# Batches 2 to 7: Q, K and x turned by TensorE in place of DMA transposes, in a fused attention and MLP kernel

## The chip, the cores and the metric

The kernel runs on one core of one Trainium2 chip. Its engines are TensorE (PE: matrix products out of SBUF into PSUM), VectorE (DVE), ScalarE (ACT), GpSimd (POOL) and SyncE (SP, which here only issues DMAs). Each engine works through its own queue in order, and they wait for each other through semaphores. The metric is device time in microseconds (us) of one execution, taken as the median of a few runs. A profile is one execution more, with every instruction's start and duration.

## The reference

Block-causal attention over 8 batches of 8 heads, 576 tokens and 64 dimensions, and then a gated MLP on the joined heads of all 4608 tokens:

```
scores = q @ k.T / sqrt(64)            # masked: block_i >= block_j, blocks of 64
attn   = softmax(scores);  a = attn @ v
x      = a.transpose(0, 2, 1, 3).reshape(4608, 512)
h      = x @ w_in                      # 512 -> 2048
g      = h * sigmoid(beta * h)
out    = g @ w_out                     # 2048 -> 512, float32
```

## The kernel before

**Attention.** The work is cut into 32 units u = 4 * batch + c, one for each batch and pair of heads. TensorE contracts over the partitions, so Q and K must stand with the head dimension on the partitions (tile `QKT`), while they arrive with tokens there. For each unit: scores (line 818, two heads at a time on the two halves of the array), Exp on ScalarE (lines 839 and 854), small memsets on VectorE for the mask, attention times V with a column of ones for the row sums (`fav`, line 882), a reciprocal and a multiplication on VectorE (lines 894 and 901, the normalisation) into `xq`. Then `xq`, with tokens on the partitions, is turned into `xT`, with features on the partitions, which is what the MLP needs.

**How Q and K are turned.** Batches 0 and 1 (`b < QB`) load Q and K in pieces (`fl`, line 711), cast them to bf16 on GpSimd (two on VectorE; line 718), turn them with TensorE into a PSUM bank (line 727, four transposes a piece; the 64 tokens left over in lines 656 and 688) and copy them to `QKT` on VectorE (line 735). Batches 2 to 7 load half a batch's heads at once (line 749), cast in four steps on GpSimd (lines 763 and 767) and turn all of it with one DMA transpose that SP issues (line 774): 2816 columns of 128, which is 22 blocks of 128 x 128.

**How x is turned.** Batches 0 to 2 (`b < XB`) use five TensorE transposes a unit (line 930) and a copy (VectorE in line 940; ScalarE in line 938 for units 2 and 3). Batches 3 to 7 use DMA transposes that SP issues (line 918, one or two a unit, as the ring `xT` wraps).

**MLP.** Nine chunks of 512 rows. For each, 16 products of 512 columns (`fh`, line 1119, four matmuls each), Tanh on ScalarE (line 1129), and the gate on VectorE (line 1133, SCALAR_TENSOR_TENSOR). The product with `w_out` is plain for chunk 0 (line 1155), and for chunks 1 to 8 made from seven products of half size (line 1040) with additions on VectorE (line 1004).

**What sets the order.** Nothing is ordered by hand. A list scheduler (`Plan.schedule`, line 85) simulates the engines at build time with a cost for each step (`dur`, `lat`), and takes on each engine the ready step of the lowest priority number. The resulting order is fixed in the program, with the semaphores that it needs (`assign`). Further fields of a step steer it: `after` (not before that other step has been placed), `rest` (a margin behind its inputs), `tiles` (buffers that must be free: class `P1` is one of eight PSUM banks, `PP` a pair of them). Up to 50 us of planned time, TensorE's gaps are filled with idle matmuls that compute nothing that is used (lines 446 and 534). MLP chunks interleave with the attention of later batches: attention of batch b runs ahead of the chunks by the offset `LAG` in `pr(u)`, line 441.

Attention matmuls and MLP matmuls share TensorE, and the copies out of PSUM share VectorE and ScalarE with the gate and the softmax.

Of the kernel before, what the change touches and what calls it, by code (L numbers as in the profile page):

```python
# [10 lines left out]
B, H, S, D = 8, 8, 576, 64  # L11
# [348 lines left out]
def bass_blockwise_causal_attn__then__act_swish_beta_kernel(  # L360
# [10 lines left out]
    with es:  # L371
# [1 line left out]
            return es.enter_context(nc.sbuf_tensor(name, shape, dt))  # L373

        NQ = 2
        QB, XB, CAST = 2, 3, "POOL"
        NE = 3
        PARTS = [((0, 4, "SP", (4, 5, 0, 1, 2, 3)), (4, 8, "SP", range(2)), (4, 8, "POOL", (4, 5, 2, 3)))] + [((0, 8, "SP", range(6)),)] * 7
        GROUPS = [((0,), (1,), (2,), (3,))] + [((0, 1), (2, 3))] * 7
# [78 lines left out]
        def mk(fn):  # L458
            return lambda g, e: fn(g)
# [13 lines left out]
        for i in range(NQ):  # L473
            for h in range(2):
                vzero.append(P.op("DVE", 150, mk(lambda g, i=i, h=h: g.memset(
                    Vn[i][64 - 64 * h:128 - 64 * h, 4, h:8:2, 0:64], 0.0)), prio=-7))
                vzero.append(P.op("DVE", 300, mk(lambda g, i=i, h=h: g.memset(
                    Vs[i][64 - 64 * h:128 - 64 * h, 4, h:8:2, :], 0.0)), prio=-8))
            o = P.op("POOL", 200, mk(lambda g, i=i: g.memset(Vn[i][:, 4, :, 64:66], 0.0)), prio=-5)
            ones.append(o)  # L480
            ones.append(P.op("POOL", 200, mk(lambda g, i=i: g.memset(Vn[i][:, 0:4, :, 64:65], 1.0)), prio=-5))
            for h in range(2):
                ones.append(P.op("POOL", 100, mk(lambda g, i=i, h=h: g.memset(
                    Vn[i][64 * h:64 * h + 64, 4, h:8:2, 64:65], 1.0)), deps=[o], prio=-4))
            ones.append(P.op("POOL", 100, mk(lambda g, i=i: g.memset(Ef[i][:, 3136:3200], 0.0)), prio=-4))
        for i in range(NQ, NE + 1):
            ones.append(P.op("POOL", 100, mk(lambda g, i=i: g.memset(Ef[i][:, 3136:3200], 0.0)), prio=-4))


        bt = P.op("SP", 100, lambda g, e: [g.dma_start(betaT, moe_beta.rearrange("(j p) -> j p", p=128))],  # L490
# [112 lines left out]
            return z  # L603


        def blocks(b):
            x0 = S * b % RX
            n = min(5, (RX - x0) // 128)
            return [z for z in ((0, n, x0), (n, 5 - n, 0)) if z[1]]

        xt = []
        early6 = []
        TC = "POOL"
        QX = 2052
        QKI, QKX = 550, 3078
        for u in range(NU):
# [8 lines left out]
            if b < QB:  # L625

                if c == 0:
# [39 lines left out]
                    else:  # L667
# [21 lines left out]
                            return z  # L689

                        o = P.op("PE", 4 * 56, ft, deps=[*tails, c4], tiles=[tq, pe_], lat=4 * 56 + 170, mode="full", prio=pr(u) + .05)
                        o.rest = 700.0 if b else 0.0
                        tailc = []
                        for a in range(2):
                            def fc(g, e, pe_=pe_, td=quads[a][1], a=a):
                                y = QKT[td.slot][:, 0, 512:576]
                                y = bass.AP(y.tensor, y.offset, [y.ap[0], [1408, 2], [768, 2], [1, 64]])
                                return g.tensor_copy(y,
                                                     PSb[:, pe_.slot, 0:512].rearrange("c (w p a n) -> c a p w n", w=2, p=2, a=2)[:, a])

                            tailc.append(P.op("DVE", dve_t(256), fc, deps=[o], tiles=[pe_, quads[a][1]], prio=-5 if b < 1 else .5))
                if p == 0:
                    tn, tt_ = quads[c // 2]
                    tail = tailc[c // 2]
                turned = []
                for w, (nm, src) in enumerate((("Q", q), ("K", k))):
                    ts, pt = P.tile("ST"), P.tile("P1")
                    early6.append(ts)

                    def fl(g, e, ts=ts, src=src, b=b, c=c):  # L710
                        return [g.dma_start(STm[ts.slot].rearrange("p h j d -> p h (j d)"),
                                            src[b, 2 * c:2 * c + 2, 0:512].rearrange("h (p j) d -> p h (j d)", j=4))]

                    o = ld[nm, u] = P.op("SP", 420 if b else 500, fl, tiles=[ts], xfer=750 if b else 820, prio=u, dma=["d_S", 0, 1])
                    o.pkt = 63.0

                    def fn(g, e, ts=ts, tn=tn, p=p, w=w):
                        return g.tensor_copy(QKn[tn.slot][:, p, 768 * w:768 * w + 512].rearrange("p (j h d) -> p j h d", j=4, h=2),
                                             STm[ts.slot].rearrange("p h j d -> p j h d"))

                    onp = u not in (0, 3) or w == 1
                    o = P.op("POOL" if onp else "DVE", 620 if onp else 430, fn, deps=[o], tiles=[ts, tn],
                             prio=-40 + 3 * u if onp else -1)

                    def ft(g, e, tn=tn, pt=pt, p=p, w=w):
                        for i in range(4):
                            z = g.transpose(PSb[:, pt.slot, 128 * i:128 * i + 128],
                                            QKn[tn.slot][:, p, 768 * w + 128 * i:768 * w + 128 * i + 128], identB[:])
                        return z

                    o = P.op("PE", 4 * 56, ft, deps=[o, c4], tiles=[tn, pt, tt_], lat=4 * 56 + 170, mode="full",
                             prio=pr(u))

                    def fc(g, e, pt=pt, td=tt_, p=p, w=w):
                        return g.tensor_copy(QKT[td.slot][:, p, 768 * w:768 * w + 512].rearrange("c (p j) -> c p j", j=4),
                                             PSb[:, pt.slot, 0:512].rearrange("c (j p) -> c p j", j=4))

                    o.rest = 700.0 if b else 0.0

                    if u == 1:  # L740
                        o.after = fq0
                    turned.append(P.op("DVE", dve_t(512) + 30, fc, deps=[o], tiles=[pt, tt_], prio=-5 if b < 1 else .5))
            elif p == 0:

                for w, (nm, src) in enumerate((("Q", q), ("K", k))):
# [24 lines left out]

                        casts.append(P.op(CAST, 740 if w else 1000, fn, deps=[o], tiles=[ts, tn], prio=u))

                def ft(g, e, tn=tn, td=tt_):
                    return [g.dma_start_transpose(QKT[td.slot][:].rearrange("c a (t n) -> c (a t) n", n=128),
                                                  QKn[tn.slot][:].rearrange("p a n -> p (a n)"))]

                turned = [P.op("SP", 3500, ft, deps=casts, tiles=[tt_, tn], xfer=3762, prio=-1, dma=["d_T", 0, 1])]
            tqk, cps = tt_, turned
            more = [tail] if b < QB else []
            ex = []  # L780
# [1 line left out]
            if b not in JOIN or p == 0:  # L782
# [4 lines left out]
                for grp in visits:  # L787
# [3 lines left out]
                    def fq(g, e, pst=pst, grp=grp, tqk=tqk, b=b):  # L791
                        keep = {}
                        for (uu, g0), ps in zip(grp, pst):
# [4 lines left out]
                            for t, q0, q1, off in blocks:  # L798
# [25 lines left out]
                    o = P.op("PE", n, fq, deps=cps + (more if b or grp[0][1] > 0 else []), tiles=list({id(x): x for x in pst}.values()) + [tqk] + [tes[uu] for uu in sorted({uu for uu, _ in grp})] * (b > 0),  # L824
                             lat=n + 200, mode="row", prio=pr(u) + .2 if len(grp) == 4 else pr(u + 1) + .1 if grp[0][0] > u else
                             pr(u) + .1 + .1 * (grp[0][1] >= 2))
                    if u == 0 and grp[0][1] == 0:
                        fq0 = o
                    for (uu, g0), ps in zip(grp, pst):
# [47 lines left out]
            def fav(g, e, te=te, pv=pv, Tv=Tv, c=c):  # L877
                for h in range(2):
                    for i in range(5):
# [6 lines left out]
            av = P.op("PE", 30 * 34, fav, deps=ex + zs + load[u], tiles=[te, Tv, pv, ti, tx],  # L886
                      lat=30 * 34 + 180, mode="full", prio=pr(u)+.4 + 5 * (b < 1))

            def both(pv, n0, n1):
                a = PS[:, pv.slot, n0:n1]  # L890
                return bass.AP(a.tensor, a.offset, [a.ap[0], [512, 2], [65, 5], [1, n1 - n0]])
# [21 lines left out]
                m = P.op("DVE", dve_t(640), fm, deps=[av, r], tiles=[pv, ti, tx], prio=-6 if b < 1 else 0)  # L913
                m.same = [r]
            nrm = [m]
            if b >= XB:
                def fy(g, e, tx=tx, c=c, b=b):
                    return [g.dma_start_transpose(
                        xT[:, c, x0:x0 + 128 * n].rearrange("c (t n) -> c t n", n=128),
                        xq[xq_(tx)][:, t0:t0 + n, :].rearrange("p t n -> p (t n)")) for t0, n, x0 in blocks(b)]  # L920

                n = len(blocks(b))
                xt.append(P.op("SP", 1000 * n, fy, deps=nrm + (xt[u - 4:u - 3] if b > XB else []), tiles=[tx], xfer=855,
                               prio=-1, dma=[f"d_TX{n}_", 0, n]))
                continue
            px = P.tile("P1")

            def fx(g, e, tx=tx, px=px):
# [3 lines left out]

            xp = P.op("PE", 5 * 57, fx, deps=nrm, tiles=[tx, px], lat=5 * 57 + 170, mode="full", prio=pr(u)+.5 + 5 * (b < 1))

            def fy(g, e, px=px, c=c, b=b):
                for t0, n, x0 in pieces(b):
                    if e == "ACT":
                        z = g.activation(xT[:, c, x0:x0 + n], PSb[:, px.slot, t0:t0 + n], ACT.Copy)
                    else:
                        z = g.tensor_copy(xT[:, c, x0:x0 + n], PSb[:, px.slot, t0:t0 + n])  # L940
                return z
            xt.append(P.op("ACT" if u in (2, 3) else "DVE", 600 if u in (2, 3) else 520, fy, deps=[xp], tiles=[px], prio=-6 if u < 4 else 0))

        for o in P.ops:
            if o.idx > 40 and o.engs == ("PE",) and not o.fill and any(d.engs == ("SP",) or d.engs == ("POOL",) for d in o.deps) and not o.rest:
# [162 lines left out]
        for r in range(NRC):  # L1108
# [26 lines left out]
                gs.append(P.op("DVE", dve_t(512), fg, deps=[a] + (spare.users + spare_x.users if r == 1 else []), tiles=[ph, tt, tg], prio=0))  # L1135

            for b in range(B):
                if any((S * b + a) // RC - RX // RC == r for a in (0, S - 1 if b < XB else 639)):
                    for c in range(4):
                        xt[4 * b + c].deps += hs  # L1140

# [107 lines left out]
```

## Time and profile before

| | us |
|---|---|
| runs before (3) | 333.79, 329.07, 334.52; median 333.79 |
| profiled execution, its own time | 332.46 |
| its span, first to last instruction | 330.6 |
| SP's DMA transposes: QKT <- QKn, 12, median issue to landing | 7.2 |
| SP's DMA transposes: xT <- xq, 24, median issue to landing | 2.7 |
| TensorE transposes L727 (64) and L930 (55 of 60 with source xq), busy | 6.5 and 4.9 |
| VectorE copies L735 (16 of 512 columns), busy | 11.0 |

How to read it: a page gives for each engine the time in which one of its instructions was running, as a share of the span. A group of instructions is a line of the program, with the mean duration of one and the idle time of the engine just before it. "PEld" are TensorE's weight loads, which overlap its matmuls. "SPq" and "POOLq" are DMA-issuing instructions, whose length is that of the issue and not of the transfer. Matmuls are pipelined: one takes longer than the distance to the next.

### The profile page before, as it was taken

To read this page: it belongs to the slowest core of one execution; us is meant where nothing else is said; L and a number is where in the kernel's file an instruction comes from. 1 tells how busy PE (TensorE), PEld (TensorE's weight loads), DVE (VectorE), ACT (ScalarE), POOL (GpSimd) and SP (SyncE) were. 2 spreads that over 40 slices of the span, in tenths; PEclk is the share of its full clock that TensorE was granted. 3 is DMA by queue.
4 is the path that set the end of the run, shared out by engine and by line. 5 is a ranking of instruction groups with operands and counts; after the bars stand their busy time and mean duration, and the time that the engine had idled before them with its cause. 6 is when DMAs were issued, how large, how long until landed. Compare 5 with 4: busy or idle time off the path is not lost.

```text
span 330.6 us, 7365 instructions
## 1 busy us (share of the span) xinstructions
PE 317.3 (96%) x3062; PEld 197.5 (60%) x2979; DVE 220.3 (67%) x454; ACT 211.8 (64%) x316; POOL 91.5 (28%) x155
## 2 busy tenths in 40 slices
PE   7898999999999999999989999899999999999996
PEld 1363464435677557845655577655566766666685
DVE  5765883777754897367967684289576866666742
ACT  3857964396737976687678855676978445554521
POOL 5962290084183066003910650080000000000000
PEclk9999999999999999999999999999999999999999
DMA  7999999999899999959899999895030310111023
GB/s 221 251 227 238 205 241 197 204 260 234 187 300 215 207 229 217 234 112 217 173 180 184 235 264 205 202 209 110 0 73 2 103 34 32 33 64 35 3 92 129
DMA packets 147442, 54.20 MB, mean 164 GB/s; under 512 B 116672, under 2 KB 146896, under 8 KB 147408
## 3 DMA queue, kind: packets, MB, share of 16 engines
q1 hardware_dynamic: 132560, 40.72, 61.9%
q0 software_dynamic: 5568, 4.36, 8.4%
q10 hardware_dynamic: 9280, 8.65, 7.9%
q8 instruction: 24, 0.39, 0.5%
q14 instruction: 10, 0.08, 0.1%
HBM read 36.71 MB, written 9.44 MB: 140 GB/s over the span
## 4 chain that ended last, share of the span: by engine, by line
PE 64%; DMA 11%; SPq 8%; DVE 6%; POOL 4%; ACT 3%; issue 2%; POOLq 0%; ACTq 0%
PE PS L1119 25%; PE PS L1040 25%; SPq L560 5%; PE PS L818 5%; DMA ST<-in_q_dram 5%; PE PS L882 5%; DMA w_out<-in_moe_w_out_dram 4%; DVE gT L1133 2%; PE PS L1155 2%; ACT E L839 2%; POOL QKn L767 1%; DMA xT<-xq 1%; DVE xq L901 1%; DMA OV<-in_v_dram 1%; POOL Vn L587 1%
## 5 line engine op out<-in xcount | busy, mean ns | idle before, releaser
L1119 PE MATMUL PS<-xT,w_in 128*128 128x512 bf16 x540 | 129.9, 379 | 3.9 <-POOL QKn L763 1.1
L1129 ACT ACTIVATE th<-PS,beta 128x512 f32<-128x512 f32 x144 | 96.6, 701 | 54.4 <-PE PS L1119 49.8
L1133 DVE SCALAR_TENSOR_TENSOR gT<-th,PS 128x512 f16<-128x512 f32 x144 | 95.5, 681 | 34.9 <-ACT th L1129 34.1
L839 ACT ACTIVATE E<-PS 128x1024 bf16<-128x1024 f32 x93 | 92.1, 1031 | 14.6 <-PE PS L818 12.0
L1119 PEld LDWEIGHTS PS<-xT,w_in 128*128 128x128 bf16 x576 | 53.3, 98 | 56.9 <-DVE gT L1133 2.0
L1040 PE MATMUL PS<-w_out,gT 128*128 128x256 f16 x512 | 62.7, 273 | 0.0
L1040 PEld LDWEIGHTS PS<-w_out,gT 128*128 128x128 f16 x512 | 49.3, 98 | 11.0 <-issue 0.4
L587 POOL CAST Vn<-Vs 128x640 bf16<-128x640 f32 (+1 forms) x28 | 20.6, 734 | 101.8 <-DMA Vs<-in_v_dram 100.5
L1061 ACT ACTIVATE ost<-PS 128x512 f32<-128x512 f32 x32 | 19.2, 600 | 30.3 <-PE PS L1040 30.3
L882 PEld LDWEIGHTS PS<-Vn,E 128*128 128x128 bf16 x930 | 31.3, 97 | 5.7 <-DVE E L845 1.8
L882 PE MATMUL PS<-Vn,E 128*128 128x65 bf16 x930 | 32.5, 193 | 1.5 <-DMA xT<-xq 1.5
L818 PE MATMUL PS<-QKT 64*64 64x64 bf16 (+4 forms) x328 | 33.9, 295 | 0.0
L1040 PE MATMUL PS<-OV 128*128 128x256 f16 x256 | 32.3, 273 | 0.0
L767 POOL CAST QKn<-ST 128x384 bf16<-128x384 f32 x48 | 27.2, 594 | 5.5 <-DMA ST<-in_q_dram 2.8
L818 PEld LDWEIGHTS PS<-QKT 64*128 64x128 bf16 (+1 forms) x328 | 13.2, 96 | 25.4 <-issue 10.4
L1040 PEld LDWEIGHTS PS<-OV 128*128 128x128 f16 x256 | 24.0, 98 | 6.9 <-issue 1.9
L901 DVE TENSOR_TENSOR xq<-PS,inv 128x640 bf16<-128x640 f32 x31 | 25.3, 820 | 0.5
L1004 DVE TENSOR_TENSOR OV<-gT 128x1024 f16<-128x1024 f16 x32 | 22.6, 711 | 1.0 <-PE PS L1040 0.4
L845 DVE MEMSET E<- 64x64 uint32 x62 | 6.9, 112 | 22.0 <-ACT E L839 20.0
L1064 DVE SCALAR_TENSOR_TENSOR ost<-PS,ost 128x512 f32<-128x512 f32 x22 | 15.2, 689 | 9.0 <-PE PS L1040 4.5
L763 POOL CAST QKn<-ST 128x640 bf16<-128x640 f32 x24 | 18.8, 784 | 4.9 <-DMA ST<-in_k_dram 3.3
L1155 PE MATMUL PS<-w_out,gT 128*128 128x512 f16 x64 | 16.0, 380 | 0.5 <-DMA w_out<-in_moe_w_out_dram 0.5
(77 smaller groups left out, 185.0 us busy)
## 6 DMA issues: line engine op xcount, KB each, us to landing
out_dram<-ost ACTq DMA_DIRECT2D x32, 256.0 KB, 3.7
ST<-in_q_dram SPq DMA_DIRECT2D x12, 576.0 KB, 6.2
ST<-in_k_dram SPq DMA_DIRECT2D x12, 576.0 KB, 7.2
Vs<-in_v_dram SPq DMA_DIRECT2D x24, 256.0 KB, 4.3
ST<-in_q_dram SPq DMA_DIRECT2D x8, 256.0 KB, 6.2
ST<-in_k_dram SPq DMA_DIRECT2D x8, 256.0 KB, 6.5
w_in<-in_moe_w_in_dram POOLq DMA_DIRECT2D x4, 512.0 KB, 11.3
w_out<-in_moe_w_out_dram POOLq DMA_DIRECT2D x4, 512.0 KB, 10.6
```

Source lines behind the costliest of these rows:

```text
L587: return g.tensor_copy(Vn[t.slot][:, 0:n, g0:g1, 0:64], Vs[ts.slot][:, 0:n, g0:g1, :])
L767: z = g.tensor_copy(QKn[tn.slot][:, a, 384 * i:384 * i + 384].rearrange("p (t h d) -> p t h d", t=3, h=2), x)
L818: z = g.matmul(o, QKT[tqk.slot][r, uu % 2, 768 + 128 * t + y:768 + 128 * t + m + y], x)
L839: return g.activation(y, x, ACT.Exp, scale=0.125)
L882: z = g.matmul(o, eblk(te, t, i, h), Vn[Tv.slot][:, t, 2 * c + h, 0:65], start=(t == 0), stop=(t == i))
L901: return g.tensor_tensor(xq[xq_(tx)][:].rearrange("p i (h d) -> p h i d", h=2), both(pv, 0, 64), x, ALU.mult)
L1004: return P.op("DVE", dve_t(SZ * HC / 2), mk(lambda g: g.tensor_tensor(fo(), fx(), fy(), op)), deps=deps, tiles=tiles, prio=prio)
L1040: x = g.matmul(PS[:, pw.slot, HM * w:HM * w + HM], fa()[:, j, 128 * w:128 * w + 128], fb()[:, j, :], start=first and (pair or w == 0) and ...
L1119: z = g.matmul(PS[:, ph.slot, :], w_in[:, c, 128 * j:128 * j + 128], xT[:, c, row % RX:row % RX + RC], start=(c == 0), stop=(c == 3))
L1129: return g.activation(th[tt.slot][:], PS[:, ph.slot, :], ACT.Tanh, scale=beta[:, j:j + 1])
L1133: return g.scalar_tensor_tensor(out=gT[tg.slot][:, j, :], in0=th[tt.slot][:], scalar=1.0, in1=PS[:, ph.slot, :], op0=ALU.add, op1=ALU.mult)
L1155: z = g.matmul(PS[:, po.slot, 0:d1 - d0], gT[tg.slot][:, j, 128 * w:128 * w + 128], w_out[:, j, d0:d1], start=(j == 0), stop=(j == NJ - 1))
```

## The change

- `QKT` of batches 2 to 7: the DMA transpose goes. In its place TensorE turns the 22 blocks into three PSUM banks (8, 8 and 6 blocks, `TURN`), and VectorE, ScalarE and VectorE copy them to `QKT`.
- `xT` of batches 3 to 7: the DMA transpose goes, and with it `XB` and `blocks`; these batches take the path of line 930. The copy is on ScalarE for units of odd number from 5 on, otherwise on VectorE.
- Batch 0: the copies of x for units 0 and 1 go from VectorE to ScalarE, where those of units 2 and 3 were.
- Batch 1: the VectorE copies of its turned Q and K are planned only after the normalisation of unit 3 (`last0["m"]`); its turns rest 400 instead of 700 ns. For unit 3 too, the turn now comes after the first scores of the unit before it.
- GpSimd's memsets at the start have other planned costs; those of 155 are planned behind the first K cast.
- The dependence between `xT`'s ring and the MLP uses the last token that is written (`S - 1`) for all batches.

```diff
-        QB, XB, CAST = 2, 3, "POOL"
+        QB, CAST = 2, "POOL"
+        TURN = ((0, 8, "DVE"), (8, 16, "ACT"), (16, 22, "DVE"))
...
-            o = P.op("POOL", 200, mk(lambda g, i=i: g.memset(Vn[i][:, 4, :, 64:66], 0.0)), prio=-5)
+            o = P.op("POOL", 150, mk(lambda g, i=i: g.memset(Vn[i][:, 4, :, 64:66], 0.0)), prio=-5)
...
-                ones.append(P.op("POOL", 100, mk(lambda g, i=i, h=h: g.memset(
+                ones.append(P.op("POOL", 155, mk(lambda g, i=i, h=h: g.memset(
                     Vn[i][64 * h:64 * h + 64, 4, h:8:2, 64:65], 1.0)), deps=[o], prio=-4))
...
+                    if u == 0 and w == 1:
+                        for x in ones:
+                            if x.dur < 160:
+                                x.after = o if x.dur > 150 else None
...
-                    o.rest = 700.0 if b else 0.0
-
-                    if u == 1:
-                        o.after = fq0
+                    o.rest = 400.0 if b else 0.0
+
+                    if u in (1, 3):
+                        o.after = fqs[u - 1, 0]
                     turned.append(P.op("DVE", dve_t(512) + 30, fc, deps=[o], tiles=[pt, tt_], prio=-5 if b < 1 else .5))
+                    turned[-1].after = last0["m"] if b else None
...
-                def ft(g, e, tn=tn, td=tt_):
-                    return [g.dma_start_transpose(QKT[td.slot][:].rearrange("c a (t n) -> c (a t) n", n=128),
-                                                  QKn[tn.slot][:].rearrange("p a n -> p (a n)"))]
-
-                turned = [P.op("SP", 3500, ft, deps=casts, tiles=[tt_, tn], xfer=3762, prio=-1, dma=["d_T", 0, 1])]
+                turned = []
+                for n0, n1, eng in TURN:
+                    pt = P.tile("P1")
+
+                    def ft(g, e, tn=tn, pt=pt, n0=n0, n1=n1):
+                        x = QKn[tn.slot][:].rearrange("p a n -> p (a n)")
+                        for i in range(n0, n1):
+                            z = g.transpose(PSb[:, pt.slot, 128 * (i - n0):128 * (i - n0) + 128],
+                                            x[:, 128 * i:128 * i + 128], identB[:])
+                        return z
+
+                    n = n1 - n0
+                    o = P.op("PE", n * 56, ft, deps=casts, tiles=[tn, pt, tt_], lat=n * 56 + 170, mode="full", prio=pr(u))
+
+                    def fc(g, e, td=tt_, pt=pt, n0=n0, n1=n1):
+                        y = QKT[td.slot][:].rearrange("c a n -> c (a n)")[:, 128 * n0:128 * n1]
+                        x = PSb[:, pt.slot, 0:128 * (n1 - n0)]
+                        return g.activation(y, x, ACT.Copy) if e == "ACT" else g.tensor_copy(y, x)
+
+                    turned.append(P.op(eng, act_t(128 * n) if eng == "ACT" else dve_t(128 * n), fc, deps=[o],
+                                       tiles=[pt, tt_], prio=.5))
...
-            if b >= XB:
-                def fy(g, e, tx=tx, c=c, b=b):
-                    return [g.dma_start_transpose(
-                        xT[:, c, x0:x0 + 128 * n].rearrange("c (t n) -> c t n", n=128),
-                        xq[xq_(tx)][:, t0:t0 + n, :].rearrange("p t n -> p (t n)")) for t0, n, x0 in blocks(b)]
-
-                n = len(blocks(b))
-                xt.append(P.op("SP", 1000 * n, fy, deps=nrm + (xt[u - 4:u - 3] if b > XB else []), tiles=[tx], xfer=855,
-                               prio=-1, dma=[f"d_TX{n}_", 0, n]))
-                continue
...
+            if u == 3:
+                last0 = {"av": av, "m": m, "xp": xp}
...
-            xt.append(P.op("ACT" if u in (2, 3) else "DVE", 600 if u in (2, 3) else 520, fy, deps=[xp], tiles=[px], prio=-6 if u < 4 else 0))
+            on = "ACT" if u in (0, 1, 2, 3) or u > 4 and u % 2 else "DVE"
+            xt.append(P.op(on, 600 if on == "ACT" else 700 if b > 1 else 520, fy, deps=[xp], tiles=[px], prio=-6 if u < 4 else 0))
...
-                if any((S * b + a) // RC - RX // RC == r for a in (0, S - 1 if b < XB else 639)):
+                if any((S * b + a) // RC - RX // RC == r for a in (0, S - 1)):
```

More of the change, by code (lines that the diff above doesn't have):

```diff
@@ L478, in bass_blockwise_causal_attn__then__act_swish_beta_kernel @@
                     Vs[i][64 - 64 * h:128 - 64 * h, 4, h:8:2, :], 0.0)), prio=-8))
-            o = P.op("POOL", 200, mk(lambda g, i=i: g.memset(Vn[i][:, 4, :, 64:66], 0.0)), prio=-5)
+            o = P.op("POOL", 150, mk(lambda g, i=i: g.memset(Vn[i][:, 4, :, 64:66], 0.0)), prio=-5)
             ones.append(o)
-            ones.append(P.op("POOL", 200, mk(lambda g, i=i: g.memset(Vn[i][:, 0:4, :, 64:65], 1.0)), prio=-5))
+            ones.append(P.op("POOL", 290, mk(lambda g, i=i: g.memset(Vn[i][:, 0:4, :, 64:65], 1.0)), prio=-5))
             for h in range(2):
-                ones.append(P.op("POOL", 100, mk(lambda g, i=i, h=h: g.memset(
+                ones.append(P.op("POOL", 155, mk(lambda g, i=i, h=h: g.memset(
                     Vn[i][64 * h:64 * h + 64, 4, h:8:2, 64:65], 1.0)), deps=[o], prio=-4))
-            ones.append(P.op("POOL", 100, mk(lambda g, i=i: g.memset(Ef[i][:, 3136:3200], 0.0)), prio=-4))
+            ones.append(P.op("POOL", 190, mk(lambda g, i=i: g.memset(Ef[i][:, 3136:3200], 0.0)), prio=-4))
         for i in range(NQ, NE + 1):
-            ones.append(P.op("POOL", 100, mk(lambda g, i=i: g.memset(Ef[i][:, 3136:3200], 0.0)), prio=-4))
+            ones.append(P.op("POOL", 190, mk(lambda g, i=i: g.memset(Ef[i][:, 3136:3200], 0.0)), prio=-4))
         bt = P.op("SP", 100, lambda g, e: [g.dma_start(betaT, moe_beta.rearrange("(j p) -> j p", p=128))],
@@ L603, in pieces @@
             return z
[L606 to L609, printed above, removed]
         xt = []
         early6 = []
+        fqs, avs = {}, {}
         TC = "POOL"
+        last0 = {}
         QX = 2052
@@ L701, in bass_blockwise_causal_attn__then__act_swish_beta_kernel @@
                             tailc.append(P.op("DVE", dve_t(256), fc, deps=[o], tiles=[pe_, quads[a][1]], prio=-5 if b < 1 else .5))
+                            tailc[-1].after = last0["m"] if b else None
                 if p == 0:
@@ L736, in fc @@
                                              PSb[:, pt.slot, 0:512].rearrange("c (j p) -> c p j", j=4))
-                    o.rest = 700.0 if b else 0.0
-                    if u == 1:
-                        o.after = fq0
+                    o.rest = 400.0 if b else 0.0
+                    if u in (1, 3):
+                        o.after = fqs[u - 1, 0]
                     turned.append(P.op("DVE", dve_t(512) + 30, fc, deps=[o], tiles=[pt, tt_], prio=-5 if b < 1 else .5))
+                    turned[-1].after = last0["m"] if b else None
             elif p == 0:
@@ L826, in bass_blockwise_causal_attn__then__act_swish_beta_kernel @@
                              pr(u) + .1 + .1 * (grp[0][1] >= 2))
+                    if b < 1:
+                        fqs[u, grp[0][1]] = o
                     if u == 0 and grp[0][1] == 0:
@@ L887, in bass_blockwise_causal_attn__then__act_swish_beta_kernel @@
                       lat=30 * 34 + 180, mode="full", prio=pr(u)+.4 + 5 * (b < 1))
+            avs[u] = av
+            if u == 3:
+                for x, y in ():
+                    avs[x].after = fqs[y]
             def both(pv, n0, n1):
@@ L933, in bass_blockwise_causal_attn__then__act_swish_beta_kernel @@
             xp = P.op("PE", 5 * 57, fx, deps=nrm, tiles=[tx, px], lat=5 * 57 + 170, mode="full", prio=pr(u)+.5 + 5 * (b < 1))
+            if u == 3:
+                last0 = {"av": av, "m": m, "xp": xp}
             def fy(g, e, px=px, c=c, b=b):
```

## The prediction, made before the run

> **What bounds the kernel now.** I read the page first, for the shares and the slices; then the busy times by stage, to see which stage has room on which engine; then TensorE's own waits; then the timeline, for what one transpose costs in this kernel. From the page:
>
> ```profile
> PE 317.3 (96%) x3062; PEld 197.5 (60%) x2979; DVE 220.3 (67%) x454; ACT 211.8 (64%) x316; POOL 91.5 (28%) x155
> PE   7898999999999999999989999899999999999996
> PEclk9999999999999999999999999999999999999999
> DMA  7999999999899999959899999895030310111023
> ```
>
> Two resources look full: TensorE from the second slice to the last but one, and the DMA engines up to slice 27 (some 225 us). The change takes work from the second and gives it to the first. So the question is which one sets the time. The stages (start; batch 1; batches 2 to 7; MLP alone; end), with TensorE busy, weight loads, VectorE, ScalarE, GpSimd, granted clock, DMA share and GB/s after each stretch's length:
>
> ```profile
> 0.00:27.20 27.20, 23.29 (x323) 10.99 (x262) 16.60 (x49) 15.90 (x24) 18.94 (x47) 1.00 1.07 234
> 27.20:60.00 32.80, 31.57 (x303) 16.33 (x298) 21.72 (x52) 21.43 (x32) 11.60 (x18) 1.00 1.17 218
> 60.00:262.00 202.00, 196.91 (x1969) 123.75 (x1945) 140.74 (x289) 144.64 (x215) 60.91 (x90) 1.00 0.90 182
> 262.00:313.00 51.00, 50.68 (x342) 33.77 (x346) 35.05 (x54) 26.16 (x39) 0.00 (x0) 1.00 0.12 42
> 313.00:330.60 17.60, 14.87 (x133) 12.63 (x130) 6.23 (x12) 3.67 (x6) 0.00 (x0) 1.00 0.30 105
> ```
>
> The last full stretch has hardly any DMA and TensorE is still full, so nothing that becomes free before it can shorten it. Busy time is a union of modelled durations and may hide slack, so I counted the work instead. The weight loads are recorded completely. From 262 to 313 they are 126 of line 1119 (512 columns) and 220 of line 1040 (256 columns). The timeline spaces eight of the first 1.73 us apart and eight of the second 0.87: 0.216 and 0.109 us each, 27.2 + 24.0 = 51.2 us of work in 51.0. That stretch is full. From 60 to 262: 384 x 0.216 = 82.9; 549 x 0.109 = 59.8; 720 attention-value matmuls at 0.91 per 30 = 21.8; twelve pairs of score units at 1.80 (visits of 0.54, 0.72 and 0.54) = 21.6; 32 of line 1155 at 0.216 = 6.9; 20 transposes at 0.056 = 1.1. Together 194.1 us in 202.0. So 7.9 us of holes, and 1.2 idle before 60, are all the room that TensorE has after 27 us.
>
> The Trainium skill ("Perfetto Trace Analysis", Identifying the Most-Contended Engine) warns that matmul busy share is a poor measure of how full TensorE is, and prefers weight-load busy share, here 60%. That would leave far more room than I allow; the count above disagrees.
>
> What TensorE waited for after 27.2 us until 313:
>
> ```profile
> PE PS L882 <- DMA xT<-xq: 1.5, 1, 1.5
> PE PS L1119 <- POOL QKn L763: 1.1, 1, 1.1
> PE PS L1119 <- DVE gT L1133: 0.7, 2, 0.5
> PE PS L1119 <- issue: 0.6, 4, 0.2
> PE PS L930 <- DVE xq L901: 0.6, 1, 0.6
> ```
>
> One wait of 1.5 us is on a DMA transpose. The 1.1 us are put down to a cast that line 1119 doesn't read; the xT transposes issued just before it are the likelier cause, which is an inference. All else that the DMA queue does is hidden: GpSimd waits 100.5 us for V and nobody waits for GpSimd.
>
> **What the change adds.** The price of a transpose comes from the timeline, where one block's start and the next block's start give the cost without the pipeline's tail:
>
> ```profile
> 29.35 0.39 PE L727 MATMUL PS<-identB,QKn 128*128 128x128 bf16 x4
> 29.57 1.03 PE L1119 MATMUL PS<-xT,w_in 128*128 128x512 bf16 x4
> ```
> ```profile
> 47.63 0.44 PE L930 MATMUL PS<-identB,xq 128*128 128x128 bf16 x5
> 47.91 1.07 PE L882 MATMUL PS<-Vn,E 128*128 128x65 bf16 x30
> ```
>
> Four take 0.22 us and five 0.28, so 0.056 each at a granted clock of 1.00. Added are 22 for each half of a batch's heads, 2 halves x 6 batches = 264, and 5 for each of the 20 units of batches 3 to 7 = 100. 364 x 0.056 = **20.4 us**, on the engine that has no room.
>
> The Trainium skill ("TensorE: Matmul & The Clock Gate", Back-to-back issue gap) gives about 81 ns for a 128-column matmul in a stream of weight load and matmul pairs. By it the addition would be 29.5 us and the time some 9 us above my sum. The two blocks above are such streams and show 56.
>
> The copies out of PSUM: VectorE's xT copies took 409 ns for 512 columns and 181 for 64, so 0.51 ns a column and 148 fixed: 670 for 1024 and 540 for 768. Twelve turns make 14.5 us, ten x copies at 0.59 make 5.9: 20.4 us. ScalarE's took 597 and 218, so 1.03 us for 1024: 12.4, and ten x copies at 0.815 make 8.2: 20.6 us. Over 60 to 262, grown by 20 us, VectorE goes from 70% to 73% and ScalarE from 72% to 74%. Neither becomes the bound; what hides the copies is that TensorE has other blocks queued. If that cover goes, TensorE waits for a bank. The nearest row is line 930's own wait: 0.6 us in 8 blocks after 27 us. For 36 turning blocks and 20 x blocks that is 56/8 x 0.6 = 4.2 us at the upper end. The lower end is 0, since line 727 has no idle time after 27 us in six blocks. I take the middle, **2.1**, because both rows are of the same form. Each new turn waits on TensorE for four GpSimd casts; everything behind it on TensorE's queue would wait too. The planner holds such a step 300 ns behind its casts, and the 1.1 us above is the largest such row. It lies within the 4.2.
>
> **What it takes away.** The 36 DMA transposes leave SP's queue and the loads behind them issue earlier. On TensorE that is worth the two waits, 1.5 + 1.1 = **2.6 us**. At least the 1.5 goes; at most all 7.9 + 1.2 = 9.1 us of holes.
>
> **The start.** First MLP matmul at 27.19. VectorE, before it:
>
> ```profile
> 23.45 0.68 DVE L735 COPY QKT<-PS 128x512 bf16<-128x512 bf16 x1
> 24.05 0.21 DVE L894 RECIPROCAL inv<-PS 128x10 f32<-128x10 f32 x1
> 24.17 0.63 DVE L735 COPY QKT<-PS 128x512 bf16<-128x512 bf16 x1
> 24.72 0.81 DVE L901 TENSOR_TENSOR gT<-PS,inv 128x640 bf16<-128x640 f32 x1
> ```
>
> The fourth attention-value block ends at 23.61. Its reciprocal waits for one batch 1 copy and its multiplication for another. With both behind it, the multiplication starts near 23.9: **0.8 us** earlier, and the transposes, ScalarE's copy and the first MLP matmul follow (its w_in had landed at 22.6). Moving the copies of units 0 and 1 to ScalarE (0.71 a unit) uses its idle 3.1 us before 24.68; put ahead of the last Exp, one could cost that 0.7 back, and VectorE, relieved of 0.97, could give another 0.4. So 0.1 to 1.2. The held batch 1 copies have cover until the scores at 27.93. Memsets: four on GpSimd (0.61 us) go behind the first K cast, which starts at 5.08 after K landed at 4.7. That is at most 0.3, and the chain of waits then runs through a Q load that lands at 9.07, so 0; the pushed memsets fit into the 1.19 us for which GpSimd next waits for a Q load. The shorter hold of batch 1's turns (400 for 700) and the smaller ring dependence touch no wait that TensorE shows: 0.
>
> **Sum.** 330.6 + 20.4 + 2.1 - 2.6 - 0.8 = 349.7 of span; 332.46 - 330.6 = 1.9 lie around it: 351.6. The profiled execution was 1.3 below the median of three, inside their scatter of 329.07 to 334.52, so I leave that out. **Predicted 351.5 us**, 5.3% slower. Ends: 330.6 + 20.4 + 0 - 9.1 - 1.2 + 1.9 = 342.6, and 330.6 + 20.4 + 4.2 - 1.5 - 0.1 + 1.9 = 355.5, with the 1.3 of the median 356.8. Range 343 to 357.
>
> **Rivals.** *Banks become the bound (slower still).* Eight PSUM banks serve scores, attention values, MLP and now 56 more blocks, whose copies stand in VectorE's and ScalarE's queues behind 0.7 to 1.0 us instructions. If each block cost the 0.35 us that one wait on line 1133 cost, it would be 19.6 us instead of 2.1: 369. It decides once copies come later than the next free bank; 73% and 74% busy speak against it, and so does line 930. Chance 9%.
>
> *TensorE was held by the DMA (not slower).* If DMA traffic delayed operands so that relieved matmuls ran closer, the transposes would fit. Place: 27 to 262 us. Price: it must give 20.4 us back for no change, or 13.7 for 2%. It decides if the matmuls there are spaced over 5% wider than alone. Against it: the same spacings, 0.216 and 0.109, account for 194.1 of 202.0 us with DMA at 0.90 and for all 51.0 with 0.12. Full recovery of every hole still ends at 342.6, 2.6% slower than the median; at 30 ns a transpose it would be 333. Chance 8%.
>
> That the change doesn't do what it says is no case: both places that issue the DMA transposes go.
>
> **Chances.** Forecast 83%, banks 9%, relief 8%. A measurement tells about 2% from no change. Relief splits into 2% faster and 6% within 2%; all else is slower, 92%.
>
> **What would show it.** Some 364 more transposes on TensorE, 0.055 to 0.06 apart; TensorE still at 96% or more, with 337 us busy; the stretch of pure MLP starting some 20 us later and still at the same spacing; VectorE and ScalarE near 241 and 234 us; DMA done well before 225 us with no gain from it; the first MLP matmul near 26.4. I'm wrong if a turning block costs over 0.1 us of TensorE idle, or if the work after 27 us ran closer than counted.

## The result, and the profile after

| | us |
|---|---|
| after, 4 runs | 352.44, 353.52, 352.44, 352.97; median 352.71 |
| before, 4 runs on the same chip | 329.07 to 334.52; median 332.20 |
| ratio after / before, 95% interval | 1.0655 [1.0556, 1.0754] |
| span of the profiled execution, before and after | 330.6 and 350.6 |

The change makes the kernel slower by some 20 us. The forecast was 351.5 in a range of 343 to 357. Before scatters by 1.6% and after by 0.3%, so the later comparisons, with 7 to 19 runs of before each and medians of 332.4 to 333.5, put the distance at 19 to 20 us. They ran on four chips, between which before's median differs by 1.1 us, so a difference of that size between kernels of different experiments says little.

From the page of the changed kernel (busy time with its share, the slices, and the large DMA queue):

```profile
PE 338.3 (96%) x3420; PEld 218.0 (62%) x3346; DVE 233.6 (67%) x488; ACT 234.2 (67%) x362; POOL 88.7 (25%) x155
PE   8999999899999999999999999999999999999996
DMA  7999999999959512961089200000000100020023
q1 hardware_dynamic: 84816, 28.78, 37.1%
```

The same queue in the kernel before:

```profile
q1 hardware_dynamic: 132560, 40.72, 61.9%
```

TensorE has 21.0 us more to do and is as full as before, over a longer span. The DMA engines, busy up to slice 27 before, now have holes from slice 12 on, and q1's share fell from 61.9% to 37.1%. Nothing of that shows in the time.

Busy time by stage, cut at the first MLP matmul and where the pure MLP stretch begins (TensorE, weight loads, VectorE, ScalarE, GpSimd, granted clock, DMA share, GB/s):

```profile
26.05:60.00 33.95, 31.80 (x326) 17.39 (x320) 22.40 (x50) 24.29 (x38) 12.21 (x19) 1.00 1.15 225
60.00:282.00 222.00, 217.74 (x2302) 143.22 (x2289) 152.52 (x327) 161.84 (x250) 58.11 (x90) 1.00 0.49 113
282.00:333.00 51.00, 50.69 (x343) 33.70 (x348) 36.52 (x57) 27.16 (x42) 0.00 (x0) 1.00 0.09 32
333.00:350.60 17.60, 14.97 (x134) 12.72 (x131) 6.33 (x12) 3.67 (x6) 0.00 (x0) 1.00 0.30 106
```

The last two rows are before's last two, TensorE's 50.69 for 50.68 and 14.97 for 14.87, 20 us later. All of the difference lies ahead of them. From the first MLP matmul to the pure MLP stretch's end it was 313 - 27.19 = 285.8 us and is 333 - 26.05 = 306.95: 21.1 more, of which 364 x 0.056 = 20.4 are the new transposes. The other 0.7 is not idle time: between these two points TensorE idles 306.95 - 300.23 = 6.7 us, and 285.81 - 279.18 = 6.6 before. What it is wasn't separated. The first MLP matmul starts 1.14 us earlier: 20.4 + 0.7 - 1.1 = 20.0, the change of the span.

TensorE's own waits from 27.2 to 333 us (three more, of 0.2 to 0.4 us, left out):

```profile
PE PS L1140 <- DVE gT L1154: 2.0, 3, 1.6
PE PS L730 <- DVE gT L1154: 0.5, 1, 0.5
PE PS L1176 <- DMA w_out<-in_moe_w_out_dram: 0.4, 1, 0.4
PE PS L1140 <- ACT QKT L794: 0.4, 1, 0.4
```

The 1.5 us for a DMA transpose are gone, and so are the 1.1 that I had put down to one. One wait of 1.6 us on VectorE's gate is new. Only 0.4 us name a copy of the new turns. The turn itself, in the timeline:

```profile
97.92 1.39 PE L784 MATMUL PS<-identB,QKn 128*128 128x128 bf16 x22
99.15 1.04 PE L1061 MATMUL PS<-OV 128*128 128x256 f16 x8
```

22 transposes in 1.23 us, 0.056 each, at full clock.

### The profile page after: what moved, and what is told of

It is laid out like the page before. It is cut to its first block, busy times and chain, and to the rows that moved or that the text cites. A ratio compares the mean times of both kernels' runs of the same rounds, so it can differ in the third digit from the quotient of the medians.

```text
span 350.6 us, 8101 instructions
## 1 busy us (share of the span) xinstructions
PE 338.3 (96%) x3420; PEld 218.0 (62%) x3346; DVE 233.6 (67%) x488; ACT 234.2 (67%) x362; POOL 88.7 (25%) x155
## 3 DMA queue, kind: packets, MB, share of 16 engines
q1 hardware_dynamic: 84816, 28.78, 37.1%
## 4 chain that ended last, share of the span: by engine, by line
PE 83%; DMA 6%; DVE 4%; ACT 4%; POOL 1%; issue 1%; SPq 0%; POOLq 0%
PE PS L1140 32%; PE PS L1061 29%; PE PS L904 7%; PE PS L838 6%; DMA w_out<-in_moe_w_out_dram 4%; PE PS L947 3%; PE PS L784 2%; ACT E L861 2%; PE PS L1176 2%; DMA ST<-in_k_dram 2%; DVE OV L1005 1%; ACT th L1150 1%; PE PS L447 1%; DVE ost L1085 1%; DVE gT L1154 1%
## 5 line engine op out<-in xcount | busy, mean ns | idle before, releaser
L1061 PE MATMUL PS<-w_out,gT 128*128 128x256 f16 x512 | 63.6, 273 | 0.0
L1061 PEld LDWEIGHTS PS<-w_out,gT 128*128 128x128 f16 x512 | 48.7, 98 | 12.3 <-issue 1.1
L588 POOL CAST Vn<-Vs 128x640 bf16<-128x640 f32 (+1 forms) x28 | 23.0, 821 | 85.8 <-PE PS L904 69.6
L1082 ACT ACTIVATE ost<-PS 128x512 f32<-128x512 f32 x32 | 19.3, 602 | 20.5 <-PE PS L1061 20.5
L771 POOL CAST QKn<-ST 128x384 bf16<-128x384 f32 x48 | 23.0, 508 | 23.3 <-PE PS L784 22.2
L1025 DVE TENSOR_TENSOR OV<-gT 128x1024 f16<-128x1024 f16 x32 | 21.7, 683 | 0.3
L794 DVE COPY QKT<-PS 128x1024 bf16<-128x1024 bf16 (+1 forms) x24 | 14.4, 618 | 10.7 <-PE PS L784 10.7
L794 ACT ACTIVATE QKT<-PS 128x1024 bf16<-128x1024 bf16 x12 | 12.3, 1025 | 10.8 <-PE PS L784 10.8
L1085 DVE SCALAR_TENSOR_TENSOR ost<-PS,ost 128x512 f32<-128x512 f32 x22 | 15.1, 687 | 5.4 <-PE PS L1061 5.4
## 6 DMA issues: line engine op xcount, KB each, us to landing
w_out<-in_moe_w_out_dram POOLq DMA_DIRECT2D x4, 512.0 KB, 10.5
```

The costliest lines, as they stand in the source:

```text
L588: return g.tensor_copy(Vn[t.slot][:, 0:n, g0:g1, 0:64], Vs[ts.slot][:, 0:n, g0:g1, :])
L771: z = g.tensor_copy(QKn[tn.slot][:, a, 384 * i:384 * i + 384].rearrange("p (t h d) -> p t h d", t=3, h=2), x)
L794: return g.activation(y, x, ACT.Copy) if e == "ACT" else g.tensor_copy(y, x)
L1025: return P.op("DVE", dve_t(SZ * HC / 2), mk(lambda g: g.tensor_tensor(fo(), fx(), fy(), op)), deps=deps, tiles=tiles, prio=prio)
L1061: x = g.matmul(PS[:, pw.slot, HM * w:HM * w + HM], fa()[:, j, 128 * w:128 * w + 128], fb()[:, j, :], start=first and (pair or w == 0) and ...
```

## Experiments: the parts one by one

My theory was that the 20 us are TensorE's own time on a full TensorE. Rivals: waits for PSUM banks and copies make a good part of it; the relieved DMA queue gives time back under it. First, each part of the change alone on the kernel before.

**Start parts alone.**

```diff
+                    turned[-1].after = last0["m"] if b else None
...
-            xt.append(P.op("ACT" if u in (2, 3) else "DVE", ...
+            xt.append(P.op("ACT" if u in (0, 1, 2, 3) else "DVE", ...
```
(and the memsets' costs, the rests and `fqs`, as in the change)

> Before, with the start parts alone (copies of units 0 and 1 on ScalarE, batch 1's copies behind the fourth normalisation, memset costs, rests). My theory: the first MLP matmul starts near 26.0 us in place of 27.19, TensorE is full behind it, so the span is 1.1 us shorter (329.5 where before has 330.6). Rival: batch 1 itself is no earlier (its scores wait for loads), so the early MLP block only leaves a hole later: the first MLP matmul is early but the span is within 0.4 us of before.

Measured: ratio 0.9984 [0.9954, 1.0014], which is -0.5 us [-1.5, +0.5]. Both expectations lie inside. The profiled execution doesn't settle it either: there a K load landed late (ScalarE waited 1.4 us for it, 0.6 before), and the first MLP matmul came at 26.9. Undecided.

**Q and K alone.** Edit: the `TURN` block of the change in place of the DMA transpose of `QKT`; `XB = 3` stays.

> Before, with Q and K of batches 2 to 7 turned by TensorE and x of batches 3 to 7 still by DMA. My theory (the time is that of the transposes on a full TensorE): 264 x 0.056 = 14.8 us more, 13.5 to 16 with changed holes; ratio near 1.045. Rival (waits for PSUM banks and copies make a good part of the whole 20 us): 36 blocks that wait 0.1 to 0.35 us each, 18 to 27 us more. Rival (relief of the DMA queue gives time back): under 12 us more.

Measured: 1.0493 [1.0452, 1.0534], +16.4 us [15.1, 17.8]. That is 1.6 over the transposes' 14.8 and at the edge of my range; 36 blocks share the 1.6, far from the first rival's 0.1 to 0.35 each, and there is no sign of relief.

**x alone.**

```diff
-        QB, XB, CAST = 2, 3, "POOL"
+        QB, XB, CAST = 2, 8, "POOL"
```
(and the copies on ScalarE for odd units)

> Before, with x of batches 3 to 7 turned by TensorE and Q and K still by DMA. My theory: 100 x 0.056 = 5.6 us more, less the 1.5 us wait on a DMA transpose of xq: 4 to 5.6; ratio near 1.015. Rival (banks and copies): 20 blocks with 0.35 us of wait each on top, 11 to 13 us more. Rival (relief): 0 to 2 us more.

Measured: 1.0108 [1.0072, 1.0143], +3.6 us [2.4, 4.8], against 5.6 us of transposes. Some 2 us come back, and the wait of line 882 on the DMA transpose is no longer in the list. Sum of the three parts: -0.5 + 16.4 + 3.6 = 19.5 us; the whole change, 352.7 - 333.4 = 19.3 by the same runs of before. The parts add up, as far as each is known (to 1.0 to 1.4 us).

**The other direction.** If TensorE's time is all, more DMA transposes should help.

```diff
-        QB, XB, CAST = 2, 3, "POOL"
+        QB, XB, CAST = 2, 2, "POOL"
```
(with the start parts; in a second kernel `XB = 1`)

> The other direction: before with the start parts, and batch 2's x turned by DMA as well (20 transposes fewer on TensorE). My theory: 20 x 0.056 = 1.1 us less than the start parts alone, since TensorE is full between 60 and 262 us; about 328.4 of span if those give 1.1. Rival (the DMA queue is the second bound, at a share over 0.9 there): four more DMA transposes delay loads behind them, and the time stays or rises by 1 to 2 us.

> As the run with batch 2's x turned by DMA, but batch 1's as well (40 transposes fewer on TensorE than before). My theory: 40 x 0.056 = 2.2 us less than the start parts alone. Rival (DMA the second bound, its share 1.17 from 27 to 60 us): the loads of w_out and of batch 2 come later and TensorE waits, 2 to 6 us more than before.

Measured: 1.0082 [1.0045, 1.0120] and 1.0277 [1.0220, 1.0334], slower by 2.7 [1.5, 4.0] and 9 us, both by more than the rival had. TensorE's waits with `XB = 2`:

```profile
PE PS L1128 <- DMA xT<-xq: 5.4, 3, 2.3
PE PS L1164 <- DMA w_out<-in_moe_w_out_dram: 1.5, 2, 1.3
```

Four DMA transposes more, and MLP matmuls wait 5.4 us for such transposes, where in before TensorE waited 1.5 for one. So the kernel before stands where TensorE and the DMA queue are both just covered; moving work either way, by these steps, costs. "All else that the DMA queue does is hidden" was true of before, but with no margin. With `XB = 1` the path is less clear: TensorE's waits there are on the Exp, the normalisation and the mask (2.8, 2.3 and 2.2 us the largest) and none is on a DMA transpose, and its granted clock was 0.979 to 0.985 over a run (0.58 from 110 to 120 us of the profile). So some of the 9 us is probably slower matmuls; how much wasn't measured.

## Experiments: how much of it is TensorE's time

**Transposes doubled and nearly removed, in after's order.** In the first kernel each added transpose is emitted twice. In the second only the first block of each turn is transposed (308 of the 364 are left out), and the copies write that block in the others' place, so that they are as long as before.

```diff
-                        for i in range(n0, n1):
+                        for i in (*range(n0, n1), *range(n0, n1)):      # twice
+                        for i in range(n0, n0 + 1):                      # few
```
(likewise in line 947 for batches 3 to 7)

> After, with each added transpose emitted twice (728 instead of 364), order and copies unchanged. My theory: 364 x 0.056 = 20.4 us more, 373. Rival (banks and copies wait under it): the doubled transposes fill waiting time, 10 to 15 us more, 363 to 368.

> After, with the first block of each turn alone transposed on TensorE (56 of the 364 added transposes stay, 308 are left out; the copies write that block in place of the others, as long as before). Order and copies are those of after. My theory: 308 x 0.056 = 17.2 us less than after, 335.4. Rival (banks and copies): the waits stay with the copies, so only 5 to 10 us go, 343 to 348. Rival (relief hidden under the transposes): more than 17 us cannot go by it, but the rest would lie clearly below before plus 56 x 0.056 = 3.1 us, under 332.

Measured: 370.17 with twice as many, 17.5 us over after's 352.71, between the two expectations: 0.048 a transpose. Of the 2.9 us that are missing to 20.4, 1.8 filled holes (TensorE's idle time fell from 350.6 - 338.3 = 12.3 to 368.3 - 357.8 = 10.5 us). With 308 fewer: 346.19, only 6.5 us less. My theory had 17.2; the rival's range holds it. Upwards the time follows TensorE, downwards it doesn't. TensorE's idle time rose to 343.5 - 323.7 = 19.8 us, spread over many waits, most of them on VectorE and ScalarE:

```profile
PE PS L1145 <- DVE gT L1159: 2.9, 7, 1.6
...
PE PS L1066 <- DVE OV L1030: 1.5, 4, 0.4
PE PS L784 <- ACT xT L965: 1.3, 4, 0.4
```

**The same with an order made for it.** An order planned for long steps could be the reason. So the planner is told the true length.

```diff
-                    o = P.op("PE", n * 56, ft, ..., lat=n * 56 + 170,
+                    o = P.op("PE", 56, ft, ..., lat=56 + 170,            # few
+                    o = P.op("PE", n * 112, ft, ..., lat=n * 112 + 170,  # twice
```
(and the x turns likewise)

> As e5_few_transposes (308 of the 364 added transposes left out, the copies as long as before), but the planner is told the shorter TensorE steps and makes an order for them. My theory (the 20 us are TensorE's time; in e5 the order, made for longer steps, turned most of what was freed into idle): 17.2 us less than after, 334 to 338. Rival (the copies, the banks and the 56 blocks cost some 10 us by themselves, whatever TensorE does): 343 to 347 as in e5.

> As e6_transposes_twice (728 added transposes), but planned with their doubled cost. My theory: 364 x 0.056 = 20.4 us over after, with the holes of after kept; 370 to 374, where the unplanned order gave 370.2. Rival (after has holes of 3 us or more per 20 us of transposes that a longer step only fills): 366 to 369.

Measured: 350.13 (346.81 to 351.41) for few, 370.87 for twice. Twice is as I had it, 18.2 us over after. With few transposes my theory fell: the median is 2.6 us under after and 4 over the unplanned kernel. Not all of that is the order. The granted clock of its four runs was 0.99 and 0.995 in the three that took 349.2 to 351.4 us, and 1.00 in the one that took 346.81; all four runs of the unplanned kernel had 1.00. So at full clock an order of its own gave nothing back (346.8 and 346.2), and took nothing either. What TensorE waited for:

```profile
PE PS L784 <- ACT QKT L796: 5.7, 5, 1.4
PE PS L730 <- POOL QKn L717: 2.9, 5, 1.1
PE PS L784 <- ACT xT L966: 1.8, 2, 1.1
PE PS L1146 <- ACT QKT L796: 1.6, 2, 1.1
```

Three of the four longest rows name copies on ScalarE, and the two of line 784 are turns that wait for the copy of an earlier one. One such place in the timeline (weight loads and other work left out):

```profile
131.48 0.22 PE L784 MATMUL PS<-identB,QKn 128*128 128x128 bf16 x1
...
131.68 0.71 ACT L966 ACTIVATE xT<-PS 128x512 bf16<-128x512 bf16 x2 [0.33 <-PE PS L949]
132.23 0.68 DVE L796 COPY QKT<-PS 128x1024 bf16<-128x1024 bf16 x1
132.45 0.29 PE L784 MATMUL PS<-identB,QKn 128*128 128x128 bf16 x2 [0.75 <-ACT xT L966]
132.71 1.02 ACT L796 ACTIVATE QKT<-PS 128x1024 bf16<-128x1024 bf16 x1 [0.32 <-PE PS L784]
...
133.79 0.39 PE L784 MATMUL PS<-identB,QKn 128*128 128x128 bf16 x2 [1.06 <-ACT QKT L796]
```

TensorE turns a block and waits 0.75 and then 1.06 us until a copy on ScalarE has ended. In this program a turn can't start without a free bank, and the end of a copy frees one, so the copies pace it here.

**Longer copies.** After with its copies made in pieces of 128 columns.

```diff
-                        return g.activation(y, x, ACT.Copy) if e == "ACT" else g.tensor_copy(y, x)
+                        for i in range(0, 128 * (n1 - n0), 128):
+                            yi, xi = y[:, i:i + 128], x[:, i:i + 128]
+                            z = g.activation(yi, xi, ACT.Copy) if e == "ACT" else g.tensor_copy(yi, xi)
+                        return z
```

> After, with the three copies of each turned half batch made in pieces of 128 columns (22 copies instead of 3; by the fixed cost of a copy about 21 us more on VectorE and 11 us more on ScalarE). My theory: copies are hidden while TensorE has other blocks; 0 to 4 us more. Rival (banks and copies): each bank is held about twice as long, 10 to 20 us more.

Measured: 354.32, 1.6 us more. VectorE's busy time rose only from 233.6 to 242.9 and ScalarE's from 234.2 to 239.0, less than half of what I had estimated, so the load put on was 9.3 and 4.8 us. Within that, longer copies are nearly hidden in after.

**Shorter copies, with all and with few transposes.** Each copy of a turn writes one block; the rest of the tile keeps older values (columns never written before are set to zero once).

```diff
-                        y = QKT[td.slot][:].rearrange("c a n -> c (a n)")[:, 128 * n0:128 * n1]
-                        x = PSb[:, pt.slot, 0:128 * (n1 - n0)]
+                        y = QKT[td.slot][:].rearrange("c a n -> c (a n)")[:, 128 * n0:128 * n0 + 128]
+                        x = PSb[:, pt.slot, 0:128]
```

> As e9_few_planned, and each of the 36 copies of turned Q and K writes one block of 128 columns instead of 8 or 6 (the rest of the tile keeps older values; planned so; about 9.5 us less on VectorE and 9.4 on ScalarE). Theory of two close bounds (TensorE's time, and just under it the copies that VectorE and ScalarE must make in order): with both taken away the time falls well under e9's 350, to 337 to 342. Rival (what holds e9 is the number of turning blocks and the banks that they take): 346 to 350 as in e9.

> After, with all its transposes, and copies of one block as in e11 (planned so). Theory of two close bounds: TensorE is full, so the shorter copies give 0 to 3 us: 350 to 353. Rival (in after too the copies are what the 20 us consist of): 9 to 12 us less, 341 to 344.

Measured, with the planner told the length in all four corners (medians in us):

| added transposes | copies of turned Q, K as in after | of one block |
|---|---|---|
| 364 | 352.7 (after) | 351.2 |
| 56 | 350.1 (346.8 at a granted clock of 1.00) | 340.0 |

Fewer transposes alone give 2.6 us (some 6 at full clock, as in the unplanned kernel), shorter copies alone 1.5 (hardly more than chips differ by), both 12.7. So each is worth far more when the other is there: 5 us more at full clock, 9 by the medians. That is what two close bounds look like: TensorE's time at 351 to 353, and at 346 to 350 the copies that VectorE and ScalarE must make between the gate, the Exp and each other. The rival, that the number of turns and of banks holds the time at 346 to 350, falls: both are the same in the kernel at 340.0. TensorE's waits there for ScalarE's copies of turns are shorter:

```profile
PE PS L787 <- ACT QKT L797: 2.4, 5, 0.7
PE PS L787 <- ACT xT L967: 1.1, 2, 0.7
```

The pages agree (busy time of the kernel with few transposes and short copies, and of that with all and short):

```profile
PE 322.0 (95%) x3112; PEld 201.1 (59%) x3039; DVE 224.6 (66%) x488; ACT 223.8 (66%) x362; POOL 91.3 (27%) x167
```
```profile
PE 336.8 (97%) x3420; PEld 218.5 (63%) x3347; DVE 226.4 (65%) x488; ACT 224.7 (64%) x362; POOL 89.9 (26%) x167
```

VectorE and ScalarE do the same within 2 us, TensorE 14.8 us less, and now the span is 9.9 us shorter (338.9 and 348.8). None of these kernels beats before; the best version stays the one before, with or without the start parts.

## Why the prediction was right, and where its reasoning was not

- **The price of a transpose** (0.056 us, 20.4 in all) was right: 22 in 1.23 us after. TensorE's busy time, 338.3 us, came out near the 337 forecast. The Trainium skill ("TensorE: Matmul & The Clock Gate", Back-to-back issue gap) has 81 ns for 128 columns; no block here shows that, and by it the time would have been near 361.
- **How full TensorE was**, by count and not by busy share, was right where it mattered: 364 transposes more than after cost 17.5 to 18.2 us. Weight-load busy share, which the Trainium skill prefers ("Perfetto Trace Analysis", Identifying the Most-Contended Engine), was 60% before and 62% after, on a TensorE that had 7 us of countable holes in 222: 214.7 us of work by before's prices between 60 and 282.
- **Copies, 2.1 us**: about right as a price in after (1.5 less with short ones, 1.6 more in pieces; after's waits name the new turns' copies with 0.4), but by luck. The 4.2 whose middle it is came from line 930's wait of 0.6 us, and that row names the normalisation that writes the transpose's input (`xq`, line 901), not a bank. It was wrong as a judgement: I took 73% and 74% busy to mean that VectorE and ScalarE were far from binding. They were 69% and 73% busy from 60 to 282 us (152.52 and 161.84 of 222), and yet the runs show a bound of theirs at 346 to 350 us, 3 to 6 us below the time. The rival "banks become the bound" was, at 9%, priced as if far away, and at 369 too dear.
- So the loss is **not** TensorE's time alone. That is what fell. With 308 of the 364 left out, 13 to 17 us of the 19 stayed; the sum came out because the larger of two nearly equal bounds was the one that I added up.
- **What it takes away, 2.6 us**: x alone gave 2.0 back (5.6 less 3.6, known to 1.2), and after has neither wait; Q and K alone gave nothing back and 1.6 on top. "Nobody waits for GpSimd" was a wrong reading: SP's DMA transposes of Q and K waited 19.6 us for its casts, and TensorE's 1.1 us row names one. No term of the sum rests on it.
- **The start, 0.8 us**: the first MLP matmul of after came 1.14 earlier; alone -0.5 us of time [-1.5, +0.5], so a gain in time isn't shown.
- **TensorE held by the DMA** fell as a way to be no slower: same spacing, no gain. But the opposite move showed what I hadn't priced, that the DMA queue was full to the point where four more transposes, with 20 fewer on TensorE, cost 2.7 us.

Open: with few transposes and short copies 340.0 still lies some 7 us over before (ratio 1.0205 [1.0137, 1.0273]). 3.1 of it are the 56 transposes left; the rest (36 short copies, the x copies, the blocks' banks) wasn't separated. Why before scatters more than after wasn't tried.

## What to carry to other kernels

Add up the work on the fullest engine by counted instructions and their distance in the timeline; what lands on it is paid nearly in full (17.5 to 18.2 of 20.4 us here). To learn whether an added cost is the only one, take it away again as well as doubling it: the doubled transposes alone would have confirmed a story that the removed ones broke. A kernel that is tuned to two limits loses whichever way work is moved, and busy shares near 75% didn't show here how close the second was.

## What the runs showed of the hardware that was not expected

TensorE's granted clock dropped where it waited for copies, in the kernel with few transposes (planned): two of its stretches, with TensorE busy 7.90 and 9.00 of 10 us,

```profile
130.00:140.00 10.00, 7.90 (x53) 4.39 (x47) 5.97 (x12) 6.35 (x10) 8.70 (x15) 0.83 0.41 115
210.00:220.00 10.00, 9.00 (x72) 5.23 (x72) 4.28 (x10) 7.50 (x12) 6.98 (x12) 0.83 0.01 2
```

against 1.00 in the stretches of after. The scores behind the waits took 0.61 us where 0.39 is usual:

```profile
135.93 0.61 PE L840 MATMUL PS<-QKT 64*128 64x512 bf16 x2
136.40 0.56 PE L840 MATMUL PS<-QKT 64*128 64x448 bf16 x2
```

The second took 0.35 in after. How much waiting it takes is not settled. Waits of 0.75 and 1.06 us in a row came before the first drop, but waits of 1.44 and 1.12 us in a row from 170 to 174 us came before none:

```profile
170.00:180.00 10.00, 7.40 (x63) 4.39 (x60) 7.00 (x14) 7.86 (x11) 7.43 (x12) 1.00 0.59 139
```

So a bound by copies can cost more than its waits. In that kernel the profiled run, with a mean clock of 0.99, took 351.08 us and the one run at 1.00 took 346.81; it is one run, and the difference is an indication only.
